# Attention and two expert layers on one core: other tiles for the second batch's keys, one pool of 2 KB tiles, and a new planned order

## The chip, the cores and the metric

The kernel runs on one core of a Trainium2 chip. The metric is the device time of one execution in microseconds (us). TensorE is called PE, its weight load PEld, VectorE DVE, ScalarE ACT, GpSimd POOL and SyncE SP; SPq is SP's instruction queue, which issues nearly all DMAs.

## The reference

Three layers follow one another. For each batch `b` (4), head (8) and 576 tokens of 64 values:

```python
a = exp(phi - max(phi, axis=2)); a = a / sum(a)      # 32 memories a head
k_m, v_m = a^T @ k, a^T @ v                          # 32 x 64 each
scores = q @ k_m^T / 8; attn = softmax(scores)
out = attn @ v_m
x = out, as 2304 tokens of 512
y = (silu(x @ w_gate) * (x @ w_val)) @ w_out         # 512 -> 1536 -> 512
e = argmax(y @ w_gate2); each expert e of 8:         # at most capacity tokens
out = gate * (relu(y_e @ w1[e]) @ w2[e])             # 512 -> 1024 -> 512
```

All matrices are 32-bit floats. The kernel holds an operand as a rounded high part and a low part and takes three products of them, so that each product of the reference is three matmuls.

## The kernel before, in words

**Stages.** The four batches go in two passes P of two batches each. In a pass, batch `b` turns `phi` into memories (`powers`, lines 505 to 528, and `memories`, from 530), then takes `q` in two halves n = 0, 1 of 288 tokens through `scores` (from 602): a matmul into `psc` (L625), a transpose by DVE (L646), maximum, subtraction (L652), exponential, sum, multiplication (L663), a transpose into `af` (L675) and the split into `at` (L430, L432 are the two lines of the split helper `cut`). For half 0 of batch 0 alone the subtraction and the multiplication run on DVE; for all others on POOL. `project` (L825, tile `pm`) multiplies the values' memories by a weight tile `wgv`, `evict_memory` splits the result into `mh`, and `batch` (line 905) multiplies `mh` by `at`, six matmuls of 288 columns into `pg` and six into `pv` for each half (L927). The 12 weight tiles `ft` stand in three groups G of four. After each group `products` multiplies by `wo` into `py` (L971). Then come the routing of tokens, and eleven units of the expert stage (L1487 up, L1527 down), the last of a smaller kind.

**Loads.** A batch needs `phi` (2 x 288 KB), keys and values `kvraw` (4 x 640 KB: for each Q = 0, 1 two tiles) and `q` (2 x 576 KB). A weight tile `wgv` or `wo` comes in two loads of 512 KB as 64-bit words, which `words` (lines 729 to 752) makes into two 32-bit parts by four passes on ACT and DVE and one on POOL; the second pass P reads the finished tiles back (`reload`, L794) from where the first pass stored them (L776). For each expert unit eight loads of 512 KB follow (L1396, L1403).

**Order.** The program is written by a planner, the class `Loom`. Each piece of work is a thread (a generator) that yields either an engine and an estimated duration (`on_pe`, `on_dma`, ...), an `Event`, or `Slots`, which count the tiles of a pool. The planner takes the engine that can start first, and of the threads that can start on it then the one with the lowest rank. It emits that instruction. So each engine's instruction order is fixed when the program is built; on the chip an engine runs its instructions in that order and waits where one isn't ready. The durations decide only about the order. Ranks come from the table `RANK`: `0ph`, `0kv0`, `0q1` are the loads of batch 0, `0m0`, `0s0` its memories and scores; `l` has the rank of the loads of the 18 weight tiles and `w` that of their splitting; the rest are offsets to due times (`due`, `out_due`, a unit's `base`). `look` is how long before the DMA queue runs empty a further load may be issued.

**Tile pools.** `raw` has 2 tiles, used by `phi`, by `kvraw` of batches 1 to 3 and others; `b` has 4 (`kvraw` of batch 0, Q = 0, then `at` and others); `w8` has 5 (`kvraw` of batch 0, Q = 1, then the weight tiles). `t2k` and `mag` have 2 tiles of 2 KB a partition each.

**The two halves.** In `scores`, the tile `af` is taken by half 0, and half 1 waits until that has happened:

```python
if n == 0:
    yield xr_s
    self.af = txr([128, 2, 2 * NB], "af")
    ...
    loom.set(self.placed)
yield self.placed
```

`batch` multiplies half 0 before half 1 (`for n in range(2)`).

Of the kernel before, what the change touches and what calls it, by code (L numbers as in the profile page):

```python
# [8 lines left out]
F32 = mybir.dt.float32  # L9
# [10 lines left out]


RANK = {
    "gate": -27.6, "mh": -36.1, "mem": -23.9, "mem0": -15.0, "py": 5.5, "out": -53.1, "tables": 10.7, "warm": -9,
# [5 lines left out]
    "mh1": 5.1, "py1": 8.8, "turn": 11.1, "route": 175.3, "zeros": -14.3, "lists": -160.5, "marks": -26.8, "pick": -213.1,  # L29
# [3 lines left out]
}  # L33


# [147 lines left out]
def on_dma(kb):  # L183
    return "SP", kb / 410
# [14 lines left out]
def attention_moe_moe_kernel(  # L199
# [18 lines left out]
    E, _, FF = w1.shape  # L218
# [39 lines left out]
        return sb.tile(list(shape), dt, tag="wide", name=name, bufs=5)  # L258

    def t2k(shape, name, dt=F32):  # L260
        return sb.tile(shape, dt, tag="t2k", name=name, bufs=2)

    def kvraw(b, Q):
        shape = [128, 4, SJ, D]
        if b > 0:
            return traw(shape, "kvraw")
        return tb(shape, "kvraw", F32) if Q == 0 else w8(shape, "kvraw", F32)

    def ttv():
        return sb.tile([128, 4, 2, 128], F32R, tag="tv", name="tv", bufs=3)  # L270
# [148 lines left out]

    loom = Loom(RANK["slack"], RANK["look"])  # L420
    banks = Slots(8)
    b_s, w8_s, wr_s, wide_s, t2k_s = Slots(4), Slots(5), Slots(4), Slots(5), Slots(2)
    tv_s, mh_s, raw_s, xr_s, mag_s, sg_s, tk_s, ex_s, pm_s = (Slots(n) for n in (0, 2, 2, 2, 2, 2, 2, 1, 2))
    yh_s, gw_s = Slots(1), Slots(3)
    HH = H // 2
    NK = NB // MM
# [7 lines left out]
    class Attention:  # L434
        def __init__(self, b):
            self.b, self.odd = b, b % 2
            self.phq, self.kvq, self.qq = [Event(), Event()], [[Event(), Event()] for _ in range(2)], [Event(), Event()]
            self.turned, self.at, self.done = [Event(), Event()], [Event(), Event()], Event()
            self.left, self.spread_left, self.n_left = 4, 2, 2
            self.tks, self.q_left, self.placed = [None, None], 2, Event()  # L440
            self.pairq, self.tvq = [Event(), Event()], [Event(), Event()]
            self.ex_ready = Event()
            self.q_tile = self.s_tile = None
            self.s_left, self.s_placed = 2, Event()
            self.raws, self.qts = [[None, None], [None, None]], [None, None]

        def load(self):
            b = self.b
            if b >= 2:
                for Q in range(2):  # L450
                    yield atts[b - 1].kvq[Q][1]
            yield raw_s
            self.ph = traw([128, 2, S], "ph")
            for Q in range(2):
                yield on_dma(295)
                nc.sync.dma_start(self.ph[:, Q], phi[b, Q])
                loom.set(self.phq[Q], loom.landed)
# [5 lines left out]
            loom.set(self.ex_ready)  # L463

        def load_kv(self, Q):
            for hp in range(2 if not self.b else 0):
                yield (b_s, w8_s)[Q]
            if self.b:
                yield pair
                for hp in range(2):  # L470
                    yield raw_s
                loom.put(pair)
            for hp in range(2):
                raw = self.raws[Q][hp] = kvraw(self.b, Q).rearrange("p (t h) j d -> p t h j d", t=2)
                yield on_dma(655)
                nc.sync.dma_start(raw, kv[self.b, Q, hp])
                loom.set(self.kvq[Q][hp], loom.landed)

        def load_q(self, n):
            if self.b >= 2:  # L480
# [44 lines left out]
        def memories(self, Q, sums):  # L525
# [6 lines left out]
            for hp in range(2):  # L532
                yield on_pe(2 * SJ, 104)
                for j in range(SJ):
                    n = 128 if j == SJ - 1 else SP
                    for i in range(2):
                        c = 2 * hp + i
                        nc.tensor.matmul(  # L538
                            kvp[32 * c : 32 * c + 32],
                            self.ex[:n, Q, j, 32 * c : 32 * c + 32],  # L540
                            self.raws[Q][hp][:n, :, i, j, :],
                            start=(j == 0),
                            stop=(j == SJ - 1),
                            tile_position=(0, 32 * c),
                        )
                loom.put(raw_s if b else (b_s, w8_s)[Q])
                self.left -= 1
                if not self.left:
                    loom.put(ex_s)
# [53 lines left out]
        def scores(self, n):  # L603
# [57 lines left out]
            nc.vector.reciprocal(m2, m2)  # L661
            yield on_v2(2 * NB) if hurry else on_g(2 * NB)
            (nc.vector if hurry else nc.gpsimd).tensor_mul(s2, s1, m2.unsqueeze(2).to_broadcast([128, 2 * NK, MM]))  # L663
            if n == 0:
                yield xr_s
                self.af = txr([128, 2, 2 * NB], "af")
                if first:
                    yield b_s
                    state[b]["at"] = tb([128, 2, 2, 2 * NB], "at")
                state[b]["af"] = self.af  # L670
                loom.set(self.placed)
# [57 lines left out]
    def words(raw, dst, key, chunk):  # L729
        high = raw[:, :, 1]  # L730
        n = raw.shape[1]
        yield mag_s
        mag = sb.tile([128, n], F32, tag="mag", name="mag", bufs=2)
        val = mag.bitcast(I32)
        yield on_a(n)
        nc.scalar.activation(mag, high.bitcast(F32), AF.Copy, scale=2.0**-111)
        yield banks
        rest = bank("rest")[:, :n].bitcast(I32)
        top = raw.rearrange("p f w -> p (f w)").bitcast(U16).rearrange("p (f w) -> p f w", w=4)[:, :, 1]
        yield on_a(n)  # L740
        nc.scalar.activation(rest, top, AF.Copy, bias=2.0**-14 - 0.5, scale=2.0**-13)
        loom.put(wr_s)
        yield on_v(n)
        nc.vector.scalar_tensor_tensor(rest, val, -(1 << 31), rest, ALU.bitwise_and, ALU.bitwise_or)
        yield on_v(n)
        nc.vector.scalar_tensor_tensor(val, val, 3, rest, ALU.logical_shift_left, ALU.bitwise_or)
        loom.put(banks)
        hi, lo = dst
        src = mag.rearrange("p (a b) -> p a b", b=hi.shape[-1]) if len(hi.shape) == 3 else mag
        yield from cut(src, hi, lo, n, pool=True)  # L750
        loom.put(mag_s)
        loom.set(wparts[key][chunk])

    wtiles, wparts, wdone, wfree, stored, recalled = {}, {}, {}, {}, {}, {}

    def weights(key, rank):

        yield w8_s
        if isinstance(key, int):
            w = wtiles[0, key] = w8([128, 2, NDT, 2, 128], "wgv")  # L760
            for i in range(2):
# [18 lines left out]

    def reload(key, k):

        yield stored[key]
        if k:
            yield recalled[order[k - 1]]
# [112 lines left out]
    def batch(b):  # L898

        P, i = divmod(b, 2)  # L900
        for G in range(NG):
            for ft in range(G * FG, (G + 1) * FG):
# [9 lines left out]
                yield allotted[P, ft]  # L912
                gh = ghs[P, G][ft % FG]
                left = [2]
                for n in range(2):
                    ns = slice(n * NB, (n + 1) * NB)
                    cols = slice((2 * i + n) * NB, (2 * i + n + 1) * NB)
                    yield atts[b].at[n]
# [142 lines left out]
    def route(blk):  # L1061
# [1 line left out]
        pl = pls[blk]  # L1063
        yield listed
        yield pl_left[blk][1]
        yield mag_s
        lt = sb.tile([2 * E, RB * TC], F32, tag="mag", name="lt", bufs=2)
        yield on_a(RB * TC)
        nc.scalar.copy(lt, pl[: 2 * E, : RB * TC])
        px = pl[:, RB * TC :]  # L1070
# [1 line left out]
        for c in range(RB):  # L1072
            nc.tensor.transpose(
                px[:, c * 2 * E : (c + 1) * 2 * E], lt[:, c * TC : (c + 1) * TC], ident[: 2 * E, : 2 * E]
            )
        loom.put(mag_s)
        lg2 = small([TC, RB, 2, E], "lg2")
        yield on_v(48)
        nc.vector.tensor_copy(lg2, px[:, : RB * 2 * E].rearrange("p (c a e) -> p c a e", a=2, e=E))
# [286 lines left out]
    class Unit:  # L1366
# [19 lines left out]
        def loads(self):  # L1386
# [4 lines left out]
            for d in range(NDT):  # L1391
                yield self.base - 15 + d + RANK["w1"]
                yield wr_s
                raw = wraw([128, FF], "w1r")
                yield on_dma(524)
                nc.sync.dma_start(raw, w1[bass.ds(self.e, 1), d * 128 : d * 128 + 128].rearrange("o p f -> p (o f)"))  # L1396
                loom.spawn(self.part1(d, raw), self.base - 8 + d + RANK["w1"], loom.landed)
            for t in range(NF2 // 2):
                yield self.base + t + RANK["w2"]
                yield wr_s  # L1400
                raw = wraw([128, 2, DM], "w2r")
                yield on_dma(524)
                nc.sync.dma_start(  # L1403
                    raw, w2[bass.ds(self.e, 1), t * 256 : (t + 1) * 256].rearrange("o (g p) d -> p (o g) d", p=128)
                )
# [437 lines left out]
```

## Time and profile before

| | |
|---|---|
| median of three runs | 692.47 us (690.83 to 692.53) |
| the profiled execution | 691.38 us |
| its span, first to last instruction | 689.7 us |
| mean granted PE clock, share of full speed | 0.979 |
| busy: PE, PEld, DVE, ACT, POOL | 654.3, 602.6, 406.7, 382.4, 221.9 us |
| DMA: moved, mean rate | 132.04 MB, 191 GB/s |

A row of a timeline has the start, the time from the first start to the last end of the merged instructions, the engine, the line, the operation, out<-in, the count, and in brackets the idle time before it with what ended it. A row of a table by stretches has the stretch, its length, each engine's busy time with the count of instructions, the granted PE clock, the busy share of the 16 DMA engines and the rate in GB/s. Matmuls are pipelined and their ends are modelled, so a run of n matmuls looks a little longer than it keeps the next one waiting.

### The profile page before, as it was taken

The page shows a single profiled execution, that of the slowest core. Times are in us where ns is not written, and L with a number is a line of the kernel's source. Part 1 is how long each engine was busy: PE and PEld are TensorE (multiplying, and loading weights), DVE is VectorE, ACT ScalarE, POOL GpSimd, SP SyncE. Part 2 cuts the span into 40 slices and gives each one's busy share as a digit, 9 for nine tenths or more (in the row PEclk, how much of TensorE's full clock was granted, in tenths as well). Part 3 has the DMA queues.
Part 4 walks back from the last instruction along what each step waited for, and adds up shares of the span by engine and source line. Part 5 has one row for each costly group of instructions (what it writes and reads, how often), then busy time and mean ns, then how long its engine had stood idle before and what let it go on. Part 6 is the DMA issues. An engine that isn't in the chain of part 4 may idle for free.

```text
span 689.7 us, 12553 instructions
## 1 busy us (share of the span) xinstructions
PE 654.3 (95%) x4681; PEld 602.6 (87%) x4681; DVE 406.7 (59%) x899; ACT 382.4 (55%) x731; POOL 221.9 (32%) x230
## 2 busy tenths in 40 slices
PE   7499999999999999999999999999999999999894
PEld 5389898998998888889989988999999999999883
DVE  3778564976676569324434645967384573753631
ACT  4579996895886258446514723425454364443540
POOL 1457564552454132602402410005162230230302
PEclk9589999999999999999999999999999999999998
DMA  8978658668762252729413332337484753753521
GB/s 343 374 256 323 226 207 313 248 208 305 316 251 108 96 215 67 248 83 320 178 62 136 140 122 93 109 97 225 154 253 153 255 188 113 266 168 118 177 102 38
DMA packets 48737, 132.04 MB, mean 191 GB/s; under 512 B 7648, under 2 KB 16864, under 8 KB 44064
## 3 DMA queue, kind: packets, MB, share of 16 engines
q1 hardware_dynamic: 45440, 121.44, 51.2%
q0 software_dynamic: 3232, 9.74, 4.3%
q8 instruction: 39, 0.64, 0.4%
q14 instruction: 26, 0.21, 0.1%
HBM read 98.10 MB, written 33.33 MB: 191 GB/s over the span
## 4 chain that ended last, share of the span: by engine, by line
PE 65%; issue 16%; DVE 7%; DMA 4%; ACT 3%; POOL 3%; SPq 1%; POOLq 0%; DVEq 0%; ACTq 0%
PE py L971 19%; PE pg L927 9%; PE pv L927 9%; PE p L1487 8%; PE p L1527 7%; PE pm L825 5%; POOL out_dram L289 3%; DMA wr<-in_moe_w_gv_dram 2%; PE kvp L538 1%; DMA qt<-in_q_dram 1%; PE psc L625 1%; PE pw L1020 1%; PE pl L1030 1%; DVE mh L432 1%; DMA wr<-in_moe_w_out_dram 1%
## 5 line engine op out<-in xcount | busy, mean ns | idle before, releaser
L971 PE MATMUL py<-wo,gh 128*128 128x512 f32 x648 | 155.5, 392 | 0.0
L971 PEld LDWEIGHTS py<-wo,gh 128*128 128x128 f32 x648 | 119.2, 188 | 23.4 <-issue 0.2
L432 POOL TENSOR_TENSOR gh<-sg,gh 128x288 fp32r<-128x288 f32 x96 | 79.4, 831 | 143.0 <-ACT gh L430 141.5
L1527 PE MATMUL p<-hh,w2h 128*128 128x288 f32 x768 | 115.4, 301 | 1.0 <-DVE hh L1503 1.0
L1487 PE MATMUL p<-xt,w1h 128*128 128x288 f32 x768 | 110.8, 297 | 0.1
L1527 PEld LDWEIGHTS p<-hh,w2h 128*128 128x128 f32 x768 | 105.5, 190 | 1.5 <-DVE hh L1503 1.4
L1487 PEld LDWEIGHTS p<-xt,w1h 128*128 128x128 f32 x768 | 104.0, 188 | 0.4 <-issue 0.3
L927 PE MATMUL pg<-at,mh 128*128 128x288 f32 x576 | 95.1, 300 | 2.7 <-DVE mh L432 1.3
L927 PE MATMUL pv<-at,mh 128*128 128x288 f32 x576 | 92.6, 296 | 0.5 <-DVE sg L840 0.4
L927 PEld LDWEIGHTS pg<-at,mh 128*128 128x128 f32 x576 | 81.8, 189 | 8.2 <-DVE mh L432 2.1
L289 POOL DMA_INDIRECT out_dram<-ot,idx x24 | 39.3, 1636 | 147.3 <-DVE ot L1566 144.6
L927 PEld LDWEIGHTS pv<-at,mh 128*128 128x128 f32 x576 | 81.6, 189 | 1.8 <-DVE sg L840 0.6
L432 DVE TENSOR_TENSOR mh<-pm,mh 64x512 fp32r<-64x512 f32 (+1 forms) x88 | 60.5, 687 | 23.4 <-ACT mh L430 21.4
L840 DVE SCALAR_TENSOR_TENSOR sg<-sg,pv 128x288 f32<-128x288 f32 x96 | 43.2, 452 | 49.6 <-ACT sg L837 25.5
L1501 ACT ACTIVATE hh<-p 128x288 fp32r<-128x288 f32 x64 | 25.2, 408 | 69.5 <-PE p L1487 57.2
L430 ACT ACTIVATE mh<-pm 64x512 fp32r<-64x512 f32 (+1 forms) x88 | 51.9, 590 | 19.5 <-PE pm L825 9.0
L1503 DVE SCALAR_TENSOR_TENSOR hh<-p,hh 128x288 fp32r<-128x288 f32 x64 | 27.3, 450 | 56.3 <-ACT hh L1501 54.2
L430 ACT ACTIVATE gh<-sg 128x288 fp32r<-128x288 f32 x96 | 42.0, 442 | 25.8 <-DVE sg L840 25.3
L432 DVE TENSOR_TENSOR w2h<-w2r,w2h 128x1024 fp32r<-128x1024 f32 x34 | 40.9, 1219 | 23.3 <-ACT w2h L430 21.2
L825 PE MATMUL pm<-wgv,tv 128*128 128x256 f32 x336 | 49.1, 291 | 0.2 <-POOL wgv L432 0.2
L432 DVE TENSOR_TENSOR w1h<-w1r,w1h 128x1024 fp32r<-128x1024 f32 x36 | 43.4, 1220 | 7.6 <-ACT w1h L430 6.8
L1439 POOL DMA_INDIRECT xr<-x,idg x24 | 23.3, 972 | 75.4 <-DVE idx L1350 63.1
(215 smaller groups left out, 849.1 us busy)
## 6 DMA issues: line engine op xcount, KB each, us to landing
w1r<-in_moe_w_dram SPq DMA_DIRECT2D x36, 512.0 KB
w2r<-in_moe_w_dram SPq DMA_DIRECT2D x36, 512.0 KB
wr<-in_moe_w_gv_dram SPq DMA_DIRECT2D x24, 512.0 KB
wsc<-wgv SPq DMA_DIRECT2D x12, 1024.0 KB
wgv<-wsc SPq DMA_DIRECT2D x12, 1024.0 KB
kvraw<-in_kv_dram SPq DMA_DIRECT2D x16, 640.0 KB
wr<-in_moe_w_out_dram SPq DMA_DIRECT2D x12, 512.0 KB
osc<-wo SPq DMA_DIRECT2D x6, 1024.0 KB
```

The source lines that it names most:

```text
L289: ins = nc.gpsimd.indirect_dma_start(*args, **kwargs)
L430: nc.scalar.activation(hi, src, AF.Copy)
L432: (nc.gpsimd if pool else nc.vector).tensor_sub(lo, src, hi.bitcast(F32))
L825: nc.tensor.matmul(pm[:, Q * 256 : (Q + 1) * 256], tv[:, 2 * Q + hp, a, :], w[:, c, 2 * Q + hp], start=(k == 0 and n3 == 0), stop=(k == le ...
L840: nc.vector.scalar_tensor_tensor(sg, sg, 2.0**-16, pv[:, :NB], ALU.mult, ALU.mult)
L927: nc.tensor.matmul(pg[:, :NB], mh[:, a, Q, gv * 128 : gv * 128 + 128], at[:, Q, c, ns], start=(Q == 0 and n3 == 0), stop=(Q == 1 and n3 == 2),
L971: nc.tensor.matmul(py, gh[:, a, k * TC : (k + 1) * TC], wtiles[P, ws[j // 2]][:, j % 2, c, :], start=(j == 0 and n3 == 0), stop=(j == FG - ...
L1439: nc.gpsimd.indirect_dma_start(self.xr[:, c], None, x2[: NT // 2] if self.early else x2, bass.IndirectOffsetOnAxis(idg[:, c : c + 1], 0))
L1487: nc.tensor.matmul(p1[:, :NB], self.w1[d][:, a, f * 128 : f * 128 + 128], self.xt[d][:, c], start=(d == 0 and n3 == 0), stop=(d == NDT - 1 ...
L1501: nc.scalar.activation(dst[:, 0], p1[:, :NB], AF.Relu)
L1503: nc.vector.scalar_tensor_tensor(dst[:, 1], p1[:, :NB], 0.0, dst[:, 0].bitcast(F32), ALU.max, ALU.subtract)
L1527: nc.tensor.matmul(p2[:, :NB], self.w2[f // 2][:, f % 2, a, d * 128 : d * 128 + 128], self.hh[f][:, c], start=(f == 0 and n3 == 0), stop=( ...
```

## The change

Six things change; no arithmetic does, and the number of matmuls and of loads stays.

- `RANK` has other numbers throughout, with `slack` 0.02 for 0 and `look` 5 for 16.
- `kvraw` of batch 1, Q = 1 takes two tiles of pool `b` in place of two of `raw`; the load of a batch's `kvraw` into `raw` first waits until the batch's `phi` has its tile (`ph_in`).
- `t2k` has four tiles and serves what `mag` served.
- Either half of the scores may take `af`, and `batch` begins with the half that is ready first in the plan.
- `reload` waits until all 18 weight tiles have got a tile of pool `w8` (`taken`).
- The planner counts 700 in place of 524 for a load of expert weights.

```diff
 RANK = {
...
-    "0ph": -205.4, "0kv0": -120.5, "0kv1": -29.2, "0q0": 158.9, "0q1": -68.8, "0m0": 157.1, "0m1": 16.2, "0s0": -26.0,
-    "0s1": 16.1, "1ph": 4.2, "1kv0": 221.8, "1kv1": 59.2, "1q0": 171.4, "1q1": 113.8, "1m0": -41.4, "1m1": 33.0,
-    "1s0": -9.5, "1s1": 108.9, "2ph": 200.4, "2kv0": 171.7, "2kv1": -63.0, "2q0": 47.0, "2q1": -49.8, "2m0": 139.3,
-    "2m1": 86.2, "2s0": -67.4, "2s1": -35.0, "3ph": 39.8, "3kv0": 206.8, "3kv1": 104.0, "3q0": -64.5, "3q1": 164.2,
+    "0ph": -527.0, "0kv0": -516.7, "0kv1": -492.8, "0q0": -36.8, "0q1": -55.6, "0m0": -188.3, "0m1": -518.2, "0s0": -143.3,
+    "0s1": 398.7, "1ph": -7.5, "1kv0": -385.8, "1kv1": 21.0, "1q0": 134.9, "1q1": 385.2, "1m0": -108.8, "1m1": -192.3,
+    "1s0": -505.4, "1s1": -529.0, "2ph": -382.5, "2kv0": -60.7, "2kv1": 23.8, "2q0": -527.5, "2q1": -63.5, "2m0": 338.9,
+    "2m1": 276.3, "2s0": 39.4, "2s1": 336.8, "3ph": 336.0, "3kv0": -538.9, "3kv1": -515.5, "3q0": 202.7, "3q1": 341.9,
...
-    "l": (7.5, -5.8, 102.2, 26.6, -12.5, 28.6, 48.2, 32.6, 59.5, 76.2, 99.2, 88.4, 109.5, 114.0, 76.3, 113.8, 133.5, 172.8),
+    "l": (-194.1, -48.1, -37.1, -21.3, 32.4, 42.3, 64.4, 58.9, 93.7, 74.8, 149.8, 139.5, 198.9, 253.1, 132.4, 271.6, 155.3, 283.6),
...
     def t2k(shape, name, dt=F32):
-        return sb.tile(shape, dt, tag="t2k", name=name, bufs=2)
+        return sb.tile(shape, dt, tag="t2k", name=name, bufs=4)

     def kvraw(b, Q):
         shape = [128, 4, SJ, D]
-        if b > 0:
+        if b > 1 or (b, Q) == (1, 0):
             return traw(shape, "kvraw")
-        return tb(shape, "kvraw", F32) if Q == 0 else w8(shape, "kvraw", F32)
+        return w8(shape, "kvraw", F32) if (b, Q) == (0, 1) else tb(shape, "kvraw", F32)
...
             self.ph = traw([128, 2, S], "ph")
+            loom.set(self.ph_in)
...
         def load_kv(self, Q):
-            for hp in range(2 if not self.b else 0):
-                yield (b_s, w8_s)[Q]
-            if self.b:
+            slot = self.kv_slot(Q)
+            if slot is not raw_s:
+                for hp in range(2):
+                    yield slot
+            else:
+                yield self.ph_in
                 yield pair
...
-            if n == 0:
+            if not self.tiled:
+                self.tiled = True
                 yield xr_s
...
     def weights(key, rank):
         yield w8_s
+        untaken[0] -= 1
+        if not untaken[0]:
+            loom.set(taken)
...
     def reload(key, k):
+        yield taken
         yield stored[key]
...
-                for n in range(2):
+                for n in sorted(range(2), key=lambda n: atts[b].at[n].time or 1e9):
...
                 raw = wraw([128, FF], "w1r")
-                yield on_dma(524)
+                yield on_dma(700)
```

`words` and `route` take `t2k` tiles in place of `mag` tiles, and the load of `w2r` has the same 700.

## Rows read from the trace of the kernel before

**Rows 1.** Parts 1 and 2 of the page: busy time, and granted clock in 40 slices.
```profile
PE 654.3 (95%) x4681; PEld 602.6 (87%) x4681; DVE 406.7 (59%) x899; ACT 382.4 (55%) x731; POOL 221.9 (32%) x230
...
PEclk9589999999999999999999999999999999999998
```

**Rows 2.** Engines' busy time by stretches of 10 us at the start.
```profile
20.00:30.00 10.00, 3.72 (x14) 1.98 (x14) 6.53 (x13) 4.96 (x11) 5.10 (x4) 0.50 1.02 420
30.00:40.00 10.00, 8.58 (x61) 7.46 (x62) 8.97 (x18) 5.79 (x12) 4.12 (x4) 0.52 0.97 332
```

**Rows 3.** Timeline of the first 48 us: SP's issues of loads.
```profile
2.67 0.43 SPq L499 DMA_DIRECT2D qt<-in_q_dram  x1
3.15 1.67 SPq L476 DMA_DIRECT2D kvraw<-in_kv_dram  x2
...
4.86 0.94 SPq L726 DMA_DIRECT2D wr<-in_moe_w_gv_dram  x2
...
14.53 2.26 SPq L499 DMA_DIRECT2D qt<-in_q_dram  x3
```

**Rows 4.** The same timeline: batch 0's way to its first gate matmul.
```profile
13.33 1.29 PE L538 MATMUL kvp<-kvraw,ex 112*32 112x128 f32 x20 [0.31 <-DMA kvraw<-in_kv_dram]
...
15.51 0.71 PE L625 MATMUL psc<-qt,tk 128*64 128x288 f32 x4
...
24.32 2.19 PE L625 MATMUL psc<-qt,tk 128*64 128x288 f32 x8 [2.78 <-DMA qt<-in_q_dram]
...
31.01 3.78 PE L538 MATMUL kvp<-kvraw,ex 112*32 112x128 f32 x40 [4.50 <-DMA kvraw<-in_kv_dram]
...
34.20 1.27 POOL L432 TENSOR_TENSOR wgv<-mag,wgv 128x512 fp32r<-128x512 f32 x1 [3.98 <-ACT wgv L430]
...
35.19 0.90 DVE L432 TENSOR_TENSOR at<-af,at 128x576 fp32r<-128x576 f32 x1
...
35.53 2.72 PE L825 MATMUL pm<-wgv,tv 128*128 128x256 f32 x11 [0.22 <-POOL wgv L432]
...
36.02 1.42 POOL L432 TENSOR_TENSOR at<-af,at 128x576 fp32r<-128x576 f32 x1 [0.54 <-ACT at L430]
...
40.67 0.98 PE L927 MATMUL pg<-at,mh 128*128 128x288 f32 x6
```

**Rows 5.** Groups by line in the first 40 us: half 1's subtraction on POOL.
```profile
L652 POOL TENSOR_TENSOR sA<-sA,m 128x576 f32<-128x576 f32 x1 | 1.2, 1158 | 1.1 <-DVE m L650 1.1
```

**Rows 6.** The same timeline: DVE and POOL on two-operand passes.
```profile
17.93 1.27 POOL L432 TENSOR_TENSOR wgv<-mag,wgv 128x512 fp32r<-128x512 f32 x1 [5.23 <-ACT wgv L430]
...
27.85 1.24 DVE L652 TENSOR_TENSOR sA<-sA,m 128x576 f32<-128x576 f32 x1
...
28.44 1.78 POOL L432 TENSOR_TENSOR wgv<-mag,wgv 128x512 fp32r<-128x512 f32 x1
```

**Rows 7.** Engines' busy time in a stretch of 2 us.
```profile
40.00:42.00 2.00, 2.00 (x18) 2.00 (x17) 0.79 (x2) 1.32 (x5) 0.65 (x3) 1.00 0.95 381
```

**Rows 8.** Engines' busy time by stretches of 20 us.
```profile
40.00:60.00 20.00, 20.00 (x170) 17.33 (x169) 15.39 (x32) 16.90 (x34) 10.39 (x14) 1.00 0.71 258
60.00:80.00 20.00, 19.03 (x120) 16.99 (x118) 12.59 (x26) 19.44 (x37) 15.19 (x14) 1.00 0.81 291
80.00:100.00 20.00, 19.81 (x143) 19.29 (x144) 12.38 (x21) 19.33 (x41) 10.76 (x12) 1.00 0.49 182
```

**Rows 9.** Timeline of SP, later issues.
```profile
94.10 1.53 SPq L476 DMA_DIRECT2D kvraw<-in_kv_dram  x2
...
168.08 3.74 SPq L726 DMA_DIRECT2D wr<-in_moe_w_out_dram  x4
173.51 0.33 SPq L794 DMA_DIRECT2D wgv<-wsc  x1
```

**Rows 10.** Engines' busy time by stretches of 20 us, routing and the end.
```profile
260.00:280.00 20.00, 17.31 (x135) 15.83 (x135) 18.56 (x94) 17.29 (x31) 6.43 (x8) 1.00 0.41 134
...
640.00:660.00 20.00, 15.98 (x111) 15.55 (x110) 14.48 (x17) 11.21 (x16) 5.20 (x3) 0.94 0.69 223
```

More of the change, by code (lines that the diff above doesn't have):

```diff
@@ L22 @@
 RANK = {
-    "gate": -27.6, "mh": -36.1, "mem": -23.9, "mem0": -15.0, "py": 5.5, "out": -53.1, "tables": 10.7, "warm": -9,
[5 rows of a table removed]
-    "mh1": 5.1, "py1": 8.8, "turn": 11.1, "route": 175.3, "zeros": -14.3, "lists": -160.5, "marks": -26.8, "pick": -213.1,
[3 rows of a table removed]
+    "gate": -318.1, "mh": -66.7, "mem": -464.3, "mem0": 36.2, "py": 408.0, "out": -17.0, "tables": 252.9, "warm": -9,
[5 rows of a table added]
+    "mh1": -406.0, "py1": 7.4, "turn": -21.0, "route": -340.6, "zeros": -518.5, "lists": -509.6, "marks": -304.6, "pick": -568.4,
[3 rows of a table added]
 }
@@ L421, in attention_moe_moe_kernel @@
     banks = Slots(8)
-    b_s, w8_s, wr_s, wide_s, t2k_s = Slots(4), Slots(5), Slots(4), Slots(5), Slots(2)
-    tv_s, mh_s, raw_s, xr_s, mag_s, sg_s, tk_s, ex_s, pm_s = (Slots(n) for n in (0, 2, 2, 2, 2, 2, 2, 1, 2))
+    b_s, w8_s, wr_s, wide_s, t2k_s = Slots(4), Slots(5), Slots(4), Slots(5), Slots(4)
+    tv_s, mh_s, raw_s, xr_s, sg_s, tk_s, ex_s, pm_s = (Slots(n) for n in (0, 2, 2, 2, 2, 2, 1, 2))
     yh_s, gw_s = Slots(1), Slots(3)
@@ L441, in __init__ @@
             self.pairq, self.tvq = [Event(), Event()], [Event(), Event()]
-            self.ex_ready = Event()
+            self.ex_ready, self.ph_in, self.tiled = Event(), Event(), False
             self.q_tile = self.s_tile = None
@@ L477, in load_kv, with kv_slot @@
                 loom.set(self.kvq[Q][hp], loom.landed)
+        def kv_slot(self, Q):
+            return raw_s if self.b > 1 or (self.b, Q) == (1, 0) else w8_s if (self.b, Q) == (0, 1) else b_s
         def load_q(self, n):
@@ L545, in memories @@
                         )
-                loom.put(raw_s if b else (b_s, w8_s)[Q])
+                loom.put(self.kv_slot(Q))
                 self.left -= 1
@@ L731, in words @@
         n = raw.shape[1]
-        yield mag_s
-        mag = sb.tile([128, n], F32, tag="mag", name="mag", bufs=2)
+        yield t2k_s
+        mag = t2k([128, n], "mag")
         val = mag.bitcast(I32)
@@ L750, in words @@
         yield from cut(src, hi, lo, n, pool=True)
-        loom.put(mag_s)
+        loom.put(t2k_s)
         loom.set(wparts[key][chunk])
     wtiles, wparts, wdone, wfree, stored, recalled = {}, {}, {}, {}, {}, {}
+    untaken, taken = [NFT + 2 * NG], Event()
     def weights(key, rank):
         yield w8_s
+        untaken[0] -= 1
+        if not untaken[0]:
+            loom.set(taken)
         if isinstance(key, int):
@@ L1065, in route @@
         yield pl_left[blk][1]
-        yield mag_s
-        lt = sb.tile([2 * E, RB * TC], F32, tag="mag", name="lt", bufs=2)
+        yield t2k_s
+        lt = t2k([2 * E, RB * TC], "lt")
         yield on_a(RB * TC)
@@ L1075, in route @@
             )
-        loom.put(mag_s)
+        loom.put(t2k_s)
         lg2 = small([TC, RB, 2, E], "lg2")
@@ L1401, in loads @@
                 raw = wraw([128, 2, DM], "w2r")
-                yield on_dma(524)
+                yield on_dma(700)
                 nc.sync.dma_start(
```

6 rows, old and new, of the table RANK are left out of this document.

## The prediction

> **What bounds the kernel now.** I read the page first. PE is busy 95% of the span [rows 1], so a new order can win only where PE stands idle, runs at the low clock or waits inside its runs. The clock row has one deep dip, in the second and third of 40 slices, about 17 to 52 us. So the next view is the table by stretches of the start. From 20 to 30 us PE is busy 3.72 of 10 us at a granted clock of 0.50, from 30 to 40 us 8.58 at 0.52 [rows 2]: the lower of the two levels, 1.2 GHz in place of 2.4, after a stretch with little work. In those 20 us the DMA engines are busy throughout (1.02 and 0.97, 420 and 332 GB/s). The early loss is thus a matter of which bytes come first.
>
> The timeline says which were late. The first real work, the gate matmul of batch 0, begins at 40.67 us [rows 4]. It needs `mh`, which comes from the first finished weight tile, and `at`. The last piece of that weight tile is split on POOL at 34.20 and done at 35.47; the matmul `pm` begins right behind it (0.22 us idle, ended by that POOL pass). `at` is done at 35.19 + 0.90 = 36.09 for half 0 and at 36.02 + 1.42 = 37.44 for half 1. Both inputs are late for the same reason. One half of `q` was issued at 2.67 us and used at 15.51, but the other was among three issued from 14.53 [rows 3] and landed only at 24.32, where PE had waited 2.78 us for it [rows 4]. That late half has to open `af`, so the early half's result lay waiting. And at 31.01 PE waits 4.50 us for keys of batch 1, which stand in its fixed order ahead of batch 0's weights.
>
> **The change part by part.** *Loads, by their new ranks.* SP takes `phi` (-527), the keys of batch 0 (-517, -493), the first weight tile (-194), `q` half 1 (-56), the second and third weight tile (-48, -37), `q` half 0 (-37), and only then `phi` of batch 1 (-8) and its keys. Before, the last keys of batch 0 landed at 13.33 [rows 4], with one `q` load of 0.59 MB issued ahead of them [rows 3]. Without it they land 0.59 MB / 420 GB/s = 1.4 us sooner, at 11.9. Two loads of the first weight tile (1.05 MB, 2.5 us) land by 14.4, `q` half 1 by 15.8, and half 0, behind two further weight loads (2.5 us) and its own 1.4, by 19.7. The instructions of SP are the same in number. `look` 5 in place of 16 makes them leave later, so that a load that has just become possible isn't behind a 16 us backlog; its cost is nothing as long as the queue has 5 us of work, and about 1.4 us a time (one load) if it once runs dry.
>
> *The half that leads.* From the first `psc` of half 0 to its finished `at` the trace shows 36.09 - 24.32 = 11.8 us [rows 4], with its arithmetic on DVE. Half 1 runs these passes on POOL, where the subtraction takes 1.16 us [rows 5] against 1.24 on DVE [rows 6]: I take 11.8 for it too. It begins when its `q` has landed, 15.8, and ends at 27.6. The bounds: not under 26, since the passes alone have to run one after another; not over 15.8 + (37.44 - 15.51) = 37.7, which is the time that half 1 took before, with its wait for the other half in it. The first weight tile lands at 14.4; its splitting is done by about 20, and `pm` and its eviction by 25. So the first gate matmul stands at 28 in place of 40.67: 12.7 us sooner.
>
> *What of that is kept.* Before 40.67 PE also did the 40 key matmuls of batch 1 (3.78 us at the low clock [rows 4], so 1.9 at the full one), which will now come later: -1.9. The clock: before, PE was dense from 31 us on and the full clock stood from 40 on [rows 2, 7], so some 8 us at half speed, 4 us lost, ahead of the first gate matmul. In the new order a part of this comes behind it; I put 3 us, with bounds of 0 and 4. Further, PE must be fed from 28 on: batch 0 has four weight tiles, each with 12 `pm` (2.9 us even at the low clock, 11 in 2.72 [rows 4]) and 24 gate matmuls (4 x 0.98), 20 to 27 us of work, in which the inputs of batch 1 can land. Before, PE was busy 39.0 of the 40 us behind 40 [rows 8]; I put 1.8 us of new small stalls, between 0 and 6. Sum: 12.7 - 1.9 - 3 - 1.8 = **6.0 us**. Its ends: start at 26, no cost, 12.8 us; start at 37.7, minus 1.9 and 6, a loss of 5 us.
>
> *A rule against it.* POOL's split of a weight took 1.27 us at 17.93 and 1.78 at 28.44, where DVE's two-operand subtraction (27.85 to 29.09) covered its first 0.65 us [rows 6]: 0.51 us longer. The Trainium skill, "SBUF — State Buffer", "Summary: rules for kernel authors", says that a DVE instruction with two inputs in SBUF and a GpSimd one that reads SBUF exclude each other, the second waiting until the first is done. This row agrees. By that rule the leading half, now the one on POOL, could be held by each such DVE pass of the other half: an estimate of up to 1.24 us for each of three POOL passes, 3.7 us, and the gain would be 2.3 us. The sum keeps 6.0, since half 0 comes four us later and meets the other's last passes alone.
>
> *Other edits.* The two tiles of pool `b` for batch 1's keys are free in this stretch, because batch 0's keys need two of four and `at` is taken when those are done; they let these keys go without a wait for both `raw` tiles. One pool of four 2 KB tiles holds what two of two held: nothing, unless `words` takes all four while a `kvs` waits (one splitting, below 5 us, inside the bound for stalls). `reload` waits for the last weight tile's slot: before, the first reload is issued at 173.51, behind the last weight loads at 168.08 to 171.82 [rows 9], so the wait ends before it is felt. If the last loads come later, what is late is the first `pm` of the second pass, by one tile of 1 MB, 2.5 us. The 700 for expert weights changes no instruction, only the order. Everything behind 100 us is ordered anew: PE loses 2.7 us in the routing and 4.0 near the end [rows 10] now, and I see no reason for either sign: 0, within 5 either way.
>
> The profiled execution took 691.38 us (span 689.7, 1.7 around it); 6.0 less is 685.4. The median of the runs is 1.1 higher, 692.47, and from it the forecast is **686.5 us**.
>
> **The rivals.** *The bytes decide anyway (same).* If PE from 28 us on catches up with the loads, it waits for batch 1's 4.4 MB or for `wo`, and by 60 us stands where it stood. For it: the DMA engines were full from 20 to 40 us [rows 2]. Against: from 40 to 60 they were busy 0.71 [rows 8], so there is room. Time: 692, within 2. That the plan doesn't bring batch 0 forward, because PE's own order still puts batch 1's keys first, would give the same.
>
> *Batches 2 and 3 push ahead (slower).* Their loads now have ranks from -382 to -539, under every weight. They become possible when batch 1's memories are made, about 40 to 50 us; before, the first keys of that kind left at 94.10 [rows 9]. Should `phi`, keys and `q` of batch 2 (4.4 MB, 10.5 us at 420 GB/s) all go ahead of `wo` and the second group of weights, PE stands for up to 10.5 us around 60 to 80 us; less the 6.0, a loss of 4.5: 697. It decides once the DMA engines have less than 10.5 us of room before those weights are due. From 40 to 100 us they had 20 x (0.29 + 0.19 + 0.51) = 20 us [rows 8], and the two `raw` tiles hold such loads back; both speak against it.
>
> *More is won (faster yet).* If the stalls of the routing and of the end [rows 10] shrink by half as well, 3.4 us, and the start wins 9, the time is 680.
>
> **How the numbers follow.** Forecast with a gain of 2 to 9 us 0.47; more 0.14; the bytes decide 0.13; slower 0.26 (batch 2's loads 0.18, other ends of the bounds 0.08). Of this kernel 0.3% is 2.1 us, about what a measurement can tell from none. Faster by more: 0.47 + 0.14 = 0.61; within: 0.13; slower: 0.26. The range that holds eight in ten runs from 677, a gain at the end of the bounds with some more behind it, to 698, batch 2's case with 1 us over; the forecast's own range is 683.5 to 690.5.
>
> **What would show it.** Right: the first gate matmul near 28 us, `q` of batch 0 landed by 20, the low clock ending by 35, PE busy over 19 of each 20 us from 40 on, and the later stages all some 6 us sooner. Wrong: a first gate matmul behind 36; or one at 28, with idle PE at 50 to 90 us that a DMA of `wr`, `kvraw` or `qt` ends; or the early gain there at 100 us and gone by the end, which would put the loss on the new order of the routing or the expert stage.

## The result, and the profile after

The changed kernel takes **698.9 us** (median of 5 runs, 697.5 to 699.34). The kernel before took 692.47 beside it (5 runs, 690.71 to 693.79). The ratio is **1.0096, with an interval of 1.0074 to 1.0118**: slower by 6.4 us. The forecast was 686.5, with 677 to 698 for the range. It had the wrong sign, and the result lies above the range.

The profiled execution took 699.14 us, its span 697.4. The page of the changed kernel gives busy time and granted clock in 40 slices, as [rows 1] do for the kernel before:

```profile
PE 658.2 (94%) x4681; PEld 604.5 (87%) x4681; DVE 407.9 (58%) x899; ACT 388.9 (56%) x735; POOL 232.2 (33%) x230
...
PEclk9699999999989999999999999999999999999997
```

The matmuls are the same 4681. The deep dip of the clock at the start is shorter: one slice with a 6, where [rows 1] have 5 and 8. A new, shallow dip (an 8) stands in the 12th slice, 192 to 209 us. The table by stretches puts sizes on both. First the kernel before, then the changed one:

```profile
0.00:100.00 100.00, 84.08 (x622) 72.91 (x623) 63.91 (x130) 76.33 (x152) 50.38 (x58) 0.90 0.77 288
100.00:180.00 80.00, 80.00 (x562) 71.10 (x562) 52.40 (x116) 58.90 (x118) 36.16 (x45) 1.00 0.78 284
180.00:224.00 44.00, 43.71 (x322) 39.19 (x321) 33.57 (x66) 34.34 (x69) 23.75 (x25) 1.00 0.52 193
```

```profile
20.00:40.00 20.00, 15.26 (x109) 12.43 (x110) 17.84 (x37) 15.96 (x30) 10.43 (x8) 0.71 1.02 405
0.00:100.00 100.00, 86.50 (x654) 76.25 (x655) 68.50 (x140) 80.55 (x160) 56.35 (x64) 0.93 0.80 302
100.00:180.00 80.00, 80.00 (x559) 70.72 (x559) 52.13 (x118) 62.24 (x123) 35.27 (x45) 1.00 0.71 257
180.00:190.00 10.00, 8.96 (x91) 8.29 (x89) 6.17 (x14) 7.56 (x16) 3.88 (x5) 1.00 0.95 350
190.00:200.00 10.00, 8.11 (x50) 6.91 (x51) 5.70 (x12) 5.75 (x14) 3.97 (x5) 0.83 0.67 253
200.00:210.00 10.00, 8.48 (x52) 7.77 (x52) 5.62 (x12) 6.49 (x13) 4.59 (x6) 0.83 0.31 131
...
220.00:230.00 10.00, 10.00 (x55) 8.36 (x55) 6.88 (x14) 5.64 (x12) 4.41 (x7) 0.86 0.36 133
180.00:224.00 44.00, 37.34 (x267) 33.99 (x266) 26.36 (x51) 29.10 (x55) 19.87 (x21) 0.88 0.53 204
```

The early gain is there: in the first 100 us PE starts 654 matmuls in place of 622. What PE loses there is its idle time and what the low clock takes from its busy time. Before, that is 15.92 + 0.10 x 84.08 = 24.3 us; after, 13.50 + 0.07 x 86.50 = 19.6, so 4.8 us are won. From 100 to 180 PE is busy throughout in both. From 180 to 224 us it is the other way round: before, PE idles 0.3 us; after, 6.7 us, and a clock of 0.88 takes another 0.12 x 37.34 = 4.5 us. That is some **11 us lost in 44**, for a gain of 4.8. (An estimate, as the clock has two decimals here.)

The marks in PE's order say the same. "To the end" is the span less the mark in the line above it.

| start of, us | before | after |
|---|---|---|
| first gate matmul | 40.67 | 36.62 |
| first `pg` behind the output matmuls of the second group | 181.7 | 180.3 |
| first output matmul of the third group | 211.1 | 224.1 |
| last output matmul of the second pass | 429.0 | 435.6 |
| span | 689.7 | 697.4 |
| to the end | 260.7 | 261.8 |

Between the second and the third mark lie 29.4 us before and 43.8 after, though the work is nearly the same: 12 more gate and value matmuls (0.16 us each) and 8 more `psc` (0.15 each) in the new order, some 3 us by the durations of before. From the last output matmul to the end, over the routing of the last tokens and the expert stage, it takes 1.1 us more; single executions of one kernel differ by more than that.

**What PE waits for there.** The view of PE's waits between 175 and 225 us of the changed kernel (us in total, times, the longest) names four:

```profile
PE psc L632 <- DMA qt<-in_q_dram: 2.9, 1, 2.9
PE pm L838 <- DVE mh L432: 2.2, 1, 2.2
PE pg L940 <- DVE mh L432: 0.8, 1, 0.8
PE pg L940 <- ACT mh L430: 0.7, 1, 0.7
```

Its timeline from 180 us, of which these rows are the chain of `mh` and the passes on the last `wo` tile ahead of it (`mag<-wr`, `rest<-wr`, `wo<-mag`):

```profile
185.71 0.66 ACT L744 ACTIVATE mag<-wr 128x512 f32<-128x512 f32 x1
186.72 0.61 ACT L749 ACTIVATE rest<-wr 128x512 int32<-128x512 uint16 x1
187.56 0.62 ACT L430 ACTIVATE wo<-mag 128x512 fp32r<-128x512 f32 x1
188.00 0.96 PE L940 MATMUL pv<-at,mh 128*128 128x288 f32 x6
188.91 0.58 ACT L430 ACTIVATE mh<-pm 64x512 fp32r<-64x512 f32 x1
189.91 0.61 ACT L430 ACTIVATE wo<-mag 128x512 fp32r<-128x512 f32 x1
190.55 1.82 ACT L430 ACTIVATE mh<-pm 64x512 fp32r<-64x512 f32 x3
191.79 2.13 DVE L432 TENSOR_TENSOR mh<-pm,mh 64x512 fp32r<-64x512 f32 x3 [1.59 <-ACT mh L430]
191.89 2.13 PE L632 MATMUL psc<-qt,tk 128*64 128x288 f32 x8 [2.93 <-DMA qt<-in_q_dram]
193.96 1.70 PE L940 MATMUL pg<-at,mh 128*128 128x288 f32 x6
...
203.80 0.54 PE L940 MATMUL pg<-at,mh 128*128 128x288 f32 x2 [0.71 <-ACT mh L430]
205.14 0.92 PE L940 MATMUL pg<-at,mh 128*128 128x288 f32 x4 [0.81 <-DVE mh L432]
```

PE ends its `pv` at 188.96. The next gate matmuls need a new `mh` of batch 0. Its tile is free when the `pv` that read the old one ends, at 185.77. But from there to 188.91 ACT runs three passes on the last `wo` tile (185.71, 186.72, 187.56; 1.9 us) and four of the gates. The first piece of `mh` is evicted at 188.91, the other three at 190.55, behind one more `wo` pass. In the program's order the first two of the four pieces are batch 0's; the second of them is done on DVE at 192.48, the first of the three that start at 191.79.

In this hole PE's fixed order has the `psc` of batch 2's second half, which waits 2.93 us for `q`. So on the chip PE waits for that DMA, and the gate matmuls follow the `psc` at 193.96. But with an earlier `q` PE would have stood before the next row instead: the `mh` came at 192.48, 0.6 us behind the `q`. Then the clock is down: six `pg` take 1.70 us at 193.96, six `pv` 0.96 at 188.00.

There are only two `mh` tiles (`mh_s` is 2), so PE has little to do while an eviction is late. It waits again at 203.80, at 205.14 and, 2.2 us long, at 219.56. There it is other work that stands ahead of the pieces or between them: at the first two passes of the gates, a table load on ACT (199.99, 1.28 us) and transposes of the scores on DVE (202.52, 203.49), at the last a pass on `m` on DVE (217.23) that took 1.26 us, where the median of its kind is 0.17. That these later waits follow from the first one is not shown.

### The profile page after: what moved, and what is told of

Same layout as the page of the kernel before. It is cut to its first block, busy times and chain, and to the rows that moved or that the text cites. A ratio compares the mean times of both kernels' runs of the same rounds, so it can differ in the third digit from the quotient of the medians.

```text
span 697.4 us, 12482 instructions
## 1 busy us (share of the span) xinstructions
PE 658.2 (94%) x4681; PEld 604.5 (87%) x4681; DVE 407.9 (58%) x899; ACT 388.9 (56%) x735; POOL 232.2 (33%) x230
## 5 line engine op out<-in xcount | busy, mean ns | idle before, releaser
L1540 PE MATMUL p<-hh,w2h 128*128 128x288 f32 x768 | 113.9, 299 | 0.0
L289 POOL DMA_INDIRECT out_dram<-ot,idx x24 | 48.9, 2036 | 146.7 <-DVE ot L1579 143.7
L1514 ACT ACTIVATE hh<-p 128x288 fp32r<-128x288 f32 x64 | 26.2, 410 | 69.0 <-PE p L1500 60.7
L850 ACT ACTIVATE sg<-pg 128x288 f32<-128x288 f32 x96 | 38.6, 407 | 28.8 <-PE pg L940 26.1
L838 PEld LDWEIGHTS pm<-wgv,tv 128*128 128x128 f32 x336 | 46.9, 207 | 7.3 <-DVE mh L432 2.6
```

Source lines behind the costliest of these rows:

```text
L289: ins = nc.gpsimd.indirect_dma_start(*args, **kwargs)
L838: nc.tensor.matmul(pm[:, Q * 256 : (Q + 1) * 256], tv[:, 2 * Q + hp, a, :], w[:, c, 2 * Q + hp], start=(k == 0 and n3 == 0), stop=(k == le ...
L850: nc.scalar.activation(sg, pg[:, :NB], AF.Silu, scale=1.0 / 256)
L1514: nc.scalar.activation(dst[:, 0], p1[:, :NB], AF.Relu)
L1540: nc.tensor.matmul(p2[:, :NB], self.w2[f // 2][:, f % 2, a, d * 128 : d * 128 + 128], self.hh[f][:, c], start=(f == 0 and n3 == 0), stop=( ...
```

## The experiments

**Theory E** was that the `mh` evictions in the third group of the first pass lose the time, because in the new plan they stand behind other work on ACT and DVE. **Rival Q** was that PE waits there because a `q` of batch 2 lands late. **Rival S** was that the new tiles and pools cost the time. **Rival W** was that the early load of the fifth `wo` tile (155.3, the 17th number of `l`) holds a `w8` slot, so that the weight tiles behind it come late. For the early part, runs 5 to 7 ask whether one edit alone carries the gain. In all of them the planner orders everything behind the edited place anew.

**1. The evictions of the third group earlier, in the changed kernel.**

```diff
-                rank = RANK["mh1" if P else "mh"] + due(b, ft)
+                rank = RANK["mh1" if P else "mh"] + due(b, ft) - (50 if not P and ft >= 8 else 0)
```

> The changed kernel, in which only the evictions of mh of the third weight group in the first pass get a rank lower by 50, so that ACT and DVE take them sooner; every engine's order up to about 165 us stays. Theory E (the 11.6 us lost between 180 and 224 us are a chain of mh evictions that stand behind other work of ACT and DVE): 686 to 692 us, the loss from 180 us to the first matmul of the next output group falls from 43.8 to about 32 us, PE's clock stays at 1.00 there. Rival Q (PE waits there because the q of batch 2 lands late, behind batch 3's keys, a reload and a store): 697 to 700, with the same wait for q near 189 us. Rival S (the new tiles and pools cost the time): 697 to 700.

Measured: **688.08 us** (10 runs, 685.35 to 690.22) beside 692.62 for the kernel before (21 runs): ratio **0.994, interval 0.9916 to 0.9963**. This one line turns a loss of 6.4 us into a gain of 4.5, and the kernel is faster than both. Its table by stretches:

```profile
0.00:100.00 100.00, 86.80 (x659) 76.68 (x660) 69.75 (x141) 81.24 (x162) 57.38 (x65) 0.93 0.80 305
100.00:180.00 80.00, 80.00 (x563) 70.83 (x562) 53.25 (x119) 63.65 (x126) 34.72 (x44) 1.00 0.73 267
180.00:224.00 44.00, 44.00 (x336) 39.22 (x335) 27.98 (x54) 30.42 (x57) 19.33 (x20) 1.00 0.59 208
```

and four rows of its timeline:

```profile
183.02 0.62 ACT L430 ACTIVATE wo<-mag 128x512 fp32r<-128x512 f32 x1
...
183.79 0.33 SPq L506 DMA_DIRECT2D qt<-in_q_dram  x1
...
185.47 1.21 ACT L430 ACTIVATE mh<-pm 64x512 fp32r<-64x512 f32 x2 [1.08 <-PE pv L940]
...
193.94 0.71 PE L632 MATMUL psc<-qt,tk 128*64 128x288 f32 x4
```

PE's busy time in the first 180 us stays as it was, within 0.3 us. From 180 to 224 PE is busy all 44 us at the full clock, and the view of its waits has no row between 175 and 225. The evictions begin at 185.47, right behind the `pv` that frees the tile, where the changed kernel has 188.91, 3.1 us behind it. The wait for `q` is gone too, though its load leaves no sooner (183.79, against 183.33 in the changed kernel): the `psc` come at 193.94, behind gate matmuls that now have their `mh`. So a late `q` alone doesn't cost the time, and rival Q falls; S falls with it.

The way to it is not the one that the edit suggests. The evictions' rank in the changed kernel is 75 to 106 (`due` gives 142 to 173 here, `mh` is -66.7), and 50 less still lies behind the -16.0 of the last `wo` tile's splitting. What the new plan does is to load that tile at 165.19 in place of 177.04, so that its last pass on ACT is done at 183.64, ahead of the moment at which the evictions can start. The order differs from about 160 us of the plan on.

The first output matmul of the third group stands at 203.7, 20.4 us sooner than in the changed kernel, the span's end 13.8 sooner (the order in between differs, so that the first number counts work that comes later here). The profiled execution is the fastest of the ten; by the medians the edit is worth 10.8 us, about the loss of the stretch.

**2. The splitting of the last `wo` tile later, in the changed kernel.** This takes away what stood ahead of the evictions on ACT, and leaves the evictions' rank alone.

```diff
-    "w": (..., 54.4, 343.2, -16.0),
+    "w": (..., 54.4, 343.2, 182.9),
```

> The changed kernel, in which only the splitting of the last output weight tile gets back the rank that it had before (182.9 for -16), so that it stands behind the mh evictions; nothing else is edited. Theory E: 686 to 692 us, as with the evictions taken first. If only the score matmuls' wait for q counts (Q): 697 to 700. S: 697 to 700.

Measured: **687.95 us** (10 runs, 687.34 to 691.32), ratio **0.9952, interval 0.9928 to 0.9977**. In its timeline the first evictions stand at 186.15 and 187.12, and the split of the last `wo` begins on ACT at 191.26 (its first passes, at 183.24 and 183.82, lie ahead of the moment at which the evictions can start). All loads up to the wait are in the order of the changed kernel, the `q` leaves at 183.61. PE is busy all of the stretch:

```profile
180.00:190.00 10.00, 10.00 (x99) 9.52 (x98) 5.79 (x13) 7.30 (x15) 2.84 (x4) 1.00 0.98 354
190.00:200.00 10.00, 10.00 (x75) 8.83 (x73) 7.09 (x13) 8.46 (x18) 6.49 (x8) 1.00 0.80 315
```

It has the same DMA share as the changed kernel there, 0.98 against 0.95 in the first ten us. So neither the bytes nor the rank of the evictions as such made the loss, but what stood ahead of them on ACT and DVE. This is the cleanest of the runs: the plan is that of the changed kernel up to 177 us.

**3. A `wo` tile loaded later, in the changed kernel (rival W).**

```diff
-    "l": (..., 132.4, 271.6, 155.3, 283.6),
+    "l": (..., 132.4, 271.6, 282.0, 283.6),
```

> The changed kernel, in which the load of the fifth output weight tile is ranked behind the last three gate-and-value tiles, as it was before, and so takes a w8 tile later. Theory W (the new order of loads leaves one w8 tile too few for the third group's weights): 690 to 694 us. Theory E: 696 to 702, since the evictions' rank is untouched.

Measured: 699.93 us (4 runs, 698.53 to 702.94), ratio 1.0132, interval 1.0076 to 1.0189: as slow as the changed kernel, where W said 690 to 694. The waits of PE for `mh` stay as well (3.4 us for ACT's part, once, and 0.5 for DVE's, between 175 and 225 us). The time alone would not decide, since the new order also has waits for `mh` near 125 us (2.9 and 1.0) that the changed kernel hasn't. But runs 1 and 2 leave the early load as it is, and the loss is gone: rival W falls with them.

**4. The evictions of the third group later, in the kernel before.** The opposite of the first run: a kernel that has none of the change's edits.

```diff
-                rank = RANK["mh1" if P else "mh"] + due(b, ft)
+                rank = RANK["mh1" if P else "mh"] + due(b, ft) + (50 if not P and ft >= 8 else 0)
```

> The kernel before, in which the mh evictions of the third weight group in the first pass get a rank higher by 50, so that they stand behind the splitting of weights and other work. Theory E: slower than the kernel before by 3 to 8 us, 695 to 700, lost between 175 and 215 us. Q, S and W: no change, 691 to 694.

Measured: **698.71 us** (6 runs, 697.54 to 699.88), ratio **1.0095, interval 1.0062 to 1.0128**. This alone costs the kernel before as much as the whole change does. The same picture appears; first its table by stretches, then PE's waits from 175 to 225 us, then its timeline:

```profile
180.00:190.00 10.00, 6.99 (x56) 5.93 (x56) 6.97 (x14) 8.22 (x16) 4.58 (x5) 0.84 0.72 277
```

```profile
PE pg L927 <- DVE mh L432: 3.8, 2, 3.0
PE pg L927 <- ACT mh L430: 0.5, 1, 0.5
```

```profile
182.41 1.28 DVE L744 SCALAR_TENSOR_TENSOR rest<-mag,rest 128x512 int32<-128x512 int32 x2
...
183.60 0.68 DVE L746 SCALAR_TENSOR_TENSOR mag<-mag,rest 128x512 int32<-128x512 int32 x1
...
185.16 2.84 DVE L432 TENSOR_TENSOR mh<-pm,mh 64x512 fp32r<-64x512 f32 x4
...
186.62 1.23 PE L927 MATMUL pg<-at,mh 128*128 128x288 f32 x4 [3.01 <-DVE mh L432]
```

To put those evictions behind other work is thus enough to lose the time, without any of the change's edits. Their rank, before between 106 and 137, is now between 156 and 187, behind the 142.5 of the fifth `wo` tile's splitting. Here it is DVE that holds them: ACT's part begins at 181.05, but on DVE passes on `wo` (182.41, 183.60, 184.56) stand ahead of the first `mh` at 185.16, and PE waits 3.01 us.

**5 to 7. The parts of the early gain.** All three start from the kernel of run 1. As each makes the planner order everything anew, their totals tell of the whole order and not of the part; the first gate matmul is what they were made for. One execution each. How far one execution can be trusted: the changed kernel and runs 1, 2, 3 and 8 have one and the same order in the first 100 us, and their first gate matmul stands at 36.62, 35.57, 36.99, 35.91 and 36.47.

Half 0 leads, as before:

```diff
-            if not self.tiled:
+            if n == 0:
...
-                for n in sorted(range(2), key=lambda n: atts[b].at[n].time or 1e9):
+                for n in range(2):
```

> Run e1's kernel, in which half 0 must again open af and is multiplied first; ranks stay. It is read at the start alone, by when the first gate matmul begins (40.67 us before, 36.62 changed). If the half that leads brings the early gain: 38.5 to 41 us. If the order of the loads brings it alone: 35.5 to 37.5 us. Behind that everything is ordered anew with ranks that were made for the other rule: slower than e1, 695 to 715 us in all.

Measured: first gate matmul at 39.59 us, total 713.87.

`look` back to its old value:

```diff
-"look": 5.0
+"look": 16.0
```

> Run e1's kernel with look 16 in place of 5, so that loads are issued up to 16 us ahead again. If it is the late commitment of the DMA queue that lets batch 0's data pass: first gate matmul at 40 us or later, and 700 to 715 us in all. If the ranks alone do it: 35.5 to 37.5 us for the first gate.

Measured: first gate matmul at 47.24, total 712.03. Its first `psc` starts at 27.78, which is 10 us and more behind that of the other kernels. The early loads leave in nearly the same order (both `q` by 10.35), but from 11.94 on `phi` and keys of batch 1 and a third `q` leave ahead of the weights that the changed kernel has there from 15.49 on.

The leading half has first place on the engines:

```diff
-    "0s1": 398.7,
+    "0s1": -600.0,
```

> Run e1's kernel with rank -600 for batch 0's half 1 of the scores in place of 398.7, so that on DVE, ACT and POOL the leading half goes ahead of the weights' splitting and of batch 1's phi. If the 18.0 us from its first score matmul to its finished at (17.08 to 35.09 us in the changed kernel) are queueing behind that other work: at of half 1 is done by 29 to 31 us and the first gate matmul begins at 30 to 33 us, where the next to bind is mh. If the chain itself takes that long: at at 34 to 36, first gate at 36 to 38. The total is not foretold, since the ranks behind are not made for it: 690 to 720 us.

Measured: first gate matmul at 36.19, where 30 to 33 had been expected, total 719.4. Its timeline:

```profile
30.44 1.75 POOL L432 TENSOR_TENSOR at<-af,at 128x576 fp32r<-128x576 f32 x1
...
32.25 0.59 ACT L430 ACTIVATE mh<-pm 128x512 fp32r<-128x512 f32 x1
...
35.35 0.69 DVE L432 TENSOR_TENSOR mh<-pm,mh 128x512 fp32r<-128x512 f32 x1
...
36.19 1.06 PE L940 MATMUL pg<-at,mh 128*128 128x288 f32 x6
```

From its first `psc` at 17.11 the leading half has its `at` done at 32.19, in 15.1 us; 29 to 31 had been expected if other work held it, 34 to 36 if the chain itself takes that long. In run 1, from which this kernel starts, it takes from 15.89 to 33.29, 17.4 us; in the changed kernel from 17.08 to 35.09, 18.0. So 2.3 to 2.9 us of the chain were other work ahead of it. But the gate matmul gains nothing that shows, since `mh` is now the later one. The `pm` of the first weight tile ended at 25.11; its eviction is done on ACT at 32.25 and on DVE at 35.35, up to 36.04. With the leading half first, it comes later on the same engines than in run 1 (30.06 and 34.34).

In run 1 the first gate matmul stands at 35.57, 5.1 us sooner than in the kernel before. Without the leading half it is at 39.59, 2.6 us and more behind the executions listed above; without the short `look` at 47.24, 10 us behind. So neither alone carries the early gain, as far as single executions of newly planned orders can tell.

**8. The old ranks for the expert stage, in the kernel of run 1**: `zeros`, `lists`, `marks`, `pick`, `w1`, `w2`, `gather`, `x`, `up`, `hidden` and `down` as before the change, and

```diff
-                yield on_dma(700)
+                yield on_dma(524)
```

> Run e1's kernel with the ranks that the kernel before has for the expert stage and the lists of tokens, and with 524 for its loads. If the new expert ranks cost what the milestones say (from the last output matmul to the end 261.8 us changed, 260.7 before): 1 us faster than e1, 686 to 688. If they are worth something behind a shifted start: 689 to 693.

Measured: 689.76 us (10 runs, 686.36 to 692.37) beside 692.32, ratio 0.9963, interval 0.9933 to 0.9992. Against run 1 nothing can be told from the times: the intervals overlap. The new ranks of the expert stage did not lose the time. Whether they win some is open: from the last output matmul to the end it is 260.7 us before, 261.8 after, 261.5 in run 1, and 264.5 in this run's profiled execution.

## Why the prediction was wrong

**The loads: right.** The order was the one read from the ranks, but for the third weight tile, which left at 15.49, behind `q` half 0 (9.98). The timeline of the changed kernel at the start:

```profile
17.08 1.42 PE L632 MATMUL psc<-qt,tk 128*64 128x288 f32 x8 [1.77 <-ACT rest L749]
...
20.99 1.23 PE L632 MATMUL psc<-qt,tk 128*64 128x288 f32 x4 [2.49 <-DMA qt<-in_q_dram]
...
22.15 2.83 PE L838 MATMUL pm<-wgv,tv 128*128 128x256 f32 x12
...
31.25 0.59 ACT L430 ACTIVATE mh<-pm 128x512 fp32r<-128x512 f32 x1
...
33.05 2.04 POOL L432 TENSOR_TENSOR at<-af,at 128x576 fp32r<-128x576 f32 x1 [1.27 <-ACT at L430]
33.06 0.75 DVE L670 TENSOR_TENSOR sA<-sA,m 128x576 f32<-128x576 f32 x1
34.24 0.65 DVE L432 TENSOR_TENSOR mh<-pm,mh 128x512 fp32r<-128x512 f32 x1
34.48 2.21 PE L545 MATMUL kvp<-kvraw,ex 112*32 112x128 f32 x40
...
36.62 1.07 PE L940 MATMUL pg<-at,mh 128*128 128x288 f32 x6
```

The first `q` was there by 17.1 us (15.8 forecast), the other by 21.0 (19.7). The wait of 4.50 us for keys of batch 1 [rows 4] is gone.

**The leading half: mis-sized.** The step said 11.8 us from its first `psc` to its `at`, and a first gate matmul at 28, 12.7 us sooner. It came at 36.62, 4.05 sooner, and the chain took 18.0. The 11.8 was measured on half 0 at a time when DVE was busy 15.50 and ACT 10.75 of 20 us [rows 2]; with weights, both halves and batch 1's `phi` all landed earlier, they are busy 17.84 and 15.96 in the same 20 to 40 us. Run 7 shows 2.3 to 2.9 us of the difference to be other work ahead of this half on its engines. The rest, 3.3 us at the least, is open; the change of engine (POOL for DVE) is in it. Of the term "`pm` and its eviction by 25" the first part held: the `pm` of the first weight tile ran from 22.15 to 24.98 (those at 31.84 are the second tile's). Its eviction did not: ACT took it at 31.25 and DVE at 34.24, behind other work, and the first `mh` was done at 34.89, ten us late. The same kind of fault comes back at 180 us. Nor did the key matmuls of batch 1 move behind the first gate matmul, for which the sum took off 1.9: `mh` was there at 34.89 and `at` at 35.09, but PE's order had those 40 first, from 34.48 on, and the gate matmul follows them at 36.62.

**What is kept: near by luck.** The forecast was 6.0 us; by the table of the first 100 us 4.8 were won, and run 1, which has this gain and no loss behind it, is 4.5 us faster than the kernel before. By the forecast's own sum a start that is 4.05 us sooner would have made a loss of 2.7. That it didn't has two reasons: the key matmuls still ran ahead of the gate matmul, and PE did other work up to 36.62. It is busy 15.26 us in the 20 from 20 to 40, at a granted clock of 0.71, where before it was 12.30 [rows 2] at 0.50 and 0.52. The size is near because errors cancel, not because the steps were right.

**The rule against it: in the row, but small.** POOL's split of the leading half's `at` took 2.04 us at 33.05, against 1.42 for the same pass in [rows 4]. DVE's two-operand pass ran beside it from 33.06 to 33.81. The starts lie 0.01 us apart, so which was second can't be told. In run 1 the same two passes meet with POOL 0.08 us ahead, and DVE's is the longer one, 1.95 us in place of 0.75; its timeline:

```profile
31.87 1.42 POOL L432 TENSOR_TENSOR at<-af,at 128x576 fp32r<-128x576 f32 x1 [1.19 <-ACT at L430]
```

```profile
31.95 1.95 DVE L670 TENSOR_TENSOR sA<-sA,m 128x576 f32<-128x576 f32 x1
```

In run 3 it is the other way round: DVE's pass starts 0.09 us ahead of POOL's, at 32.40, and takes 0.75, and POOL's takes 1.94. So the one that comes second is held: about 0.5 us for POOL, or 1.20 for DVE. By the Trainium skill, "SBUF — State Buffer", "Summary: rules for kernel authors", the two exclude each other and the second waits; the rows of runs 1 and 3 agree. On the leading half it fell on one pass, and not on three of 1.24 us as the bound had it. Nor is 1.24 what such a pass takes by itself: the same subtraction on DVE took 0.75 in the changed kernel (28.68).

**The step that failed: "Everything behind 100 us is ordered anew ... I see no reason for either sign: 0, within 5 either way".** There was a reason, and it stands in the table of ranks. The `mh` evictions of the third group are wanted at `mh` + `due`, and the splitting of the last `wo` tile went from 182.9 to -16.0, ahead of them. With two `mh` tiles a late eviction leaves PE without gate matmuls, and its fixed order then puts something else there, or nothing. The cost was 11 us of the stretch from 180 to 224, over twice the bound given. Run 2 shows it by taking it away with that one rank, run 1 by another way, and run 4 by making it in the kernel before. How the 11 us divide among the single waits is read from the trace, not tested.

**The rivals.** *Batches 2 and 3 push ahead* had the right sign and about the right time (697), but not the cause: PE's idle time from 40 to 100 us is no larger than before (0.7 us against 1.2), and the loss stands 100 us later. It had also misread the table: only batch 2's `phi` and first `q` and batch 3's keys have ranks from -382 to -539, while batch 2's keys have -60.7 and 23.8. With the rank of that `phi` or those of batch 3's keys (-538.9, -515.5) set back to the old ones, the planner writes the same program; that of the `q` changes it and was not run. *The bytes decide anyway* fell with run 1, in which the early gain reaches the end. *More is won* wasn't seen. `reload`'s new wait was put at nothing, and so it is: without it the planner writes the same program. Of what would show it wrong, two came true: "a first gate matmul behind 36", by 0.62 us, and "the early gain there at 100 us and gone by the end", only neither in the routing nor in the expert stage.

## What to carry to other kernels

When an order is planned anew, look for the tiles with the fewest copies that stand between PE and an evicting engine, and read for each what the new ranks put ahead of its eviction: that is where a gain at the start is given back. A wait that the profile puts down to a DMA may stand in a hole that another engine's chain would leave anyway: look when the input of the next row came. After an edit of a rank, read what the plan did with it, as the way may be another than the one intended. And a duration measured while engines had less to do can be too short once the change gives them more.

## What was not expected of the hardware

A short wait late in the kernel brought the clock down as the long thin stretch at the start did. PE ended at 188.96 and waited until 191.89. Read in stretches of 1 us, the granted clock was 1.00 up to 192, and 0.50, the lower of the two levels, from 192 to 195. Over the two stretches of ten us from 190 on it is 0.83 each, as it fell again behind the waits of 0.71 and 0.81 us at 203.80 and 205.14; from 220 to 230 it is 0.86, behind the wait of 2.2 us. At the lower level six matmuls of 288 columns took 1.70 us, 0.96 at the full one. Of some 11 us lost from 180 to 224, by the sum above, 4.5 are this: here the low clock adds two thirds to what the idle time itself costs. The Trainium skill, "TensorE: Matmul & The Clock Gate", "HAM oscillation — how this bites in real kernels", tells of a kernel in which PE waits some 3 to 5 us for a DMA between its tiles and begins each next tile at the lower clock. Waits of 2.93 and 2.21 us were followed by the same here.
